# Float64 weights decoded in PSUM, a square moved into the bank of h, and a start on another DMA queue

## The chip, the cores and the metric

The kernel runs on one core of one Trainium2 chip. The metric is the device time of one execution in microseconds. Five engines work side by side, each through its own instructions in a fixed order: TensorE (PE; its weight loads are shown as PEld), VectorE (DVE), ScalarE (ACT), GpSimd (POOL) and SyncE (SP), which issues DMAs. An engine whose next instruction waits for another engine holds up everything behind it in its own order.

## The reference

The program is a causal convolution over the sequence, followed by two MLPs over all 8192 tokens. There are 192 channels and 2048 hidden features, and inputs and outputs are float32; the four weight matrices of the MLPs come as float64.

```python
w = softmax(weight)                       # 8 heads x 7 taps
x = causal_conv(x, w)                     # [8192, 192], one tap row for each 24 channels
h = x @ w_in1;  g = h * clip(h + 3, 0, 6) / 6;  x = g @ w_out1      # layer 1
h = x @ w_in2                                                       # layer 2
P = a0 + a1*h + a2*h**2 + a3*h**3
Q = 1 + |b0|*|h| + |b1|*h**2
out = (P / (Q + 1e-6)) @ w_out2
```

## The kernel before, in words

Tokens go through in 16 blocks of 512 (the last in two halves); activations stay transposed, features on partitions and tokens along the free axis. Each operand of a large product is split into a high and a low part, so that a product is a sum of three: high by high, high by low and low by high. A step is one tile of 128 features: 5 matmuls into h (`mm1`, `mm3`; L464), then element-wise work, then 5 matmuls of its result into the block's accumulators (L478 to L483). In the steady state a step of layer 1 of one block runs beside a step of layer 2 of the block before it: 20 matmuls of 512 columns.

PSUM has four banks of 128x512 for h (`bank0` to `bank3`, printed as bank_93 to bank_96) and four for accumulators. Layer 1 uses banks 0 and 1, layer 2 banks 2 and 3; the second block's layer 1, which runs beside the first's, uses layer 2's banks and buffers. The bank of a step of layer 2 is free for the next product once `G` (L631) has read it.

Layer 2's element-wise work on one tile, by engine: ACT makes A = |h| (L569), in every other tile also a scaled square S (L588), and T = a3*h (L581). POOL makes S = Q - c1 (L602, with L590 ahead of it in every other tile). DVE makes the polynomial in three steps `t2` (L596), `t3` (L607) and `p2` (L626). ACT makes R, 1/sqrt(Q), into A (L612) and squares it to the estimate of 1/Q (`RR`, L617). DVE makes one Newton factor `w` (L622) and the result `G` (L631); ACT rounds it to the high part (`hi2`, L637) and POOL makes the low part (L646). Layer 1's is shorter: `u` (ACT, L506), `g` (DVE, L511), the high part (ACT, L518), the low part (POOL, L524).

The weights arrive as pairs of 32-bit words, 32 tiles of 256, 384 or 512 columns (384 in the mean), through four buffers `raw`. The leading bits of each float64 are put together as a float32 in a tile `m` of SBUF: ACT takes the magnitude of the upper word (L324), DVE clamps it (L332), shifts it (L334) and combines it with sign and lower word (L337, L339); ACT copies the high part (L346 to L355) and POOL (layer 1) or DVE (layer 2) subtracts for the low part (L363). This is done while the first two blocks go through layer 1.

The order of each engine's instructions is not that of the code. Every operation is entered with a time at which it is wanted (tables of offsets such as `OFF`), an estimated length and the buffers it reads and writes, and a planner (`Issue`) writes out one static order; `AHEAD` and `LOOK` say how far it may bring an operation forward. The program's first DMAs are all on SP's queue, the table of taps (`tap`, L840), the softmax row (`line_d`, L845) and the matrices of the convolution made from it (`band`, L266) among the loads of x and of weights.

Of the kernel before, what the change touches and what calls it, by code (L numbers as in the profile page):

```python
# [44 lines left out]
X0 = -2.88  # L45
XW = [-99.782, -93.075, -91.583, -91.01]
BIAS = dict(l1=0.05, dec=-0.28, conv=0.02, out=-0.19, x2=0.95)
AHEAD = dict(P=1.7, A=0.18, V=0.15, G=3.5, S=999)
LOOK = dict(P=29, A=172, V=0, G=1293, S=0)
OFF = dict(  # L50
    sq=0.41, q1=0.596, q2=0.698, mm3=0.072, mm1=0.147, mm4=0.184, tr=0.275, mm2=0.294, A=0.21,
    t1=0.486, u=0.487, R=0.702, RR=0.868, hi2=1.618, hi1=1.431, S=0.271, lo2=2.435, lo1=1.66,
    q=0.669, t2=0.664, t3=1.126, w=1.281, p2=1.267, G=1.367, g=0.622, cv=0.702, x1ah=0.593,
    x1al=1.068, x1bh=0.588, x1bl=0.706, x2ah=0.383, x2al=1.059, x2mh=0.864, x2mc=1.507, x2ml=1.145, oa=0.655,
    oc=0.668, os=0.526, mm2l=0.367, mm4l=0.618,
# [843 lines left out]
```

## Time and profile before

| | |
|---|---|
| median of three runs | 1367.36 us (1365.62, 1367.36, 1374.5) |
| profiled execution: its span, and its time | 1365.6 us, 1365.62 us |
| mean granted TensorE clock | 0.987 |
| busy: PE, DVE, ACT, POOL | 94%, 93%, 87%, 86% |
| first matmul; first product of layer 2 | 17.63 us; 138.25 us |

The span of the profile is the time of that execution, with nothing around it. Matmuls are pipelined, so PE's busy share says little; the distance between the starts of two matmuls says more. Three stages have different limits: the start with the weights (to about 171 us), the steady state (to about 1195 us), and the last block (to the end).

### The profile page before, as it was taken

What the parts mean: (1) busy time and instruction counts of PE and PEld (TensorE: products, weight loads), DVE (VectorE), ACT (ScalarE), POOL (GpSimd) and SP (SyncE); (2) the same over time, 40 slices, a digit from 0 to 9 for tenths busy, and PEclk for the clock granted to TensorE, in tenths of its full rate; (3) what the DMA queues carried; (4) which work ended last, traced back from release to release, by engine and by line L of the source; (5) the groups of instructions that cost most, each with busy time, mean ns of one, the idle gap of its engine ahead of it and who ended that gap; (6) DMA issues with size and microseconds to landing.
All of it is one profiled execution on the core that took longest, in us unless ns stands there. A gap on an engine that the chain in (4) does not pass through costs nothing.

```text
span 1365.6 us, 18227 instructions
## 1 busy us (share of the span) xinstructions
PE 1282.4 (94%) x6048; PEld 1041.8 (76%) x6048; DVE 1269.9 (93%) x1824; ACT 1193.1 (87%) x2174; POOL 1179.1 (86%) x932
## 2 busy tenths in 40 slices
PE   3797999999999999999999999999999999989976
PEld 3574777878788787878888878788787877877776
DVE  6999999999999999999999999999999999998897
ACT  5677899999899999989999989899898989887895
POOL 3665899999999998999989999999999998987886
PEclk9899999999999999999999999999999999999998
DMA  6232000000000000000000000000000000000000
GB/s 197 80 117 70 15 0 13 15 0 27 1 13 1 12 30 12 15 1 12 15 12 16 12 15 12 1 16 12 15 12 1 12 0 6 7 1 12 1 12 12
DMA packets 28983, 28.60 MB, mean 21 GB/s; under 512 B 2140, under 2 KB 25816, under 8 KB 28888
## 3 DMA queue, kind: packets, MB, share of 16 engines
q1 hardware_dynamic: 28888, 27.44, 6.6%
q8 instruction: 47, 0.77, 0.2%
q14 instruction: 48, 0.39, 0.1%
HBM read 21.13 MB, written 6.30 MB: 20 GB/s over the span
## 4 chain that ended last, share of the span: by engine, by line
DVE 46%; PE 33%; ACT 10%; POOL 7%; issue 4%; DMA 1%; SPq 0%; DVEq 0%; POOLq 0%; ACTq 0%
PE bank L464 16%; DVE S L622 11%; DVE bank L626 7%; DVE T L631 6%; DVE u L511 4%; DVE bank L607 4%; DVE T L596 4%; POOL S L602 3%; PE acc L481 3%; PE acc L478 3%; PE acc L479 3%; PE acc L483 3%; PE acc L482 3%; ACT A L617 2%; ACT A L612 2%
## 5 line engine op out<-in xcount | busy, mean ns | idle before, releaser
L602 POOL TENSOR_TENSOR S<-A,S 128x512 f32<-128x512 f32 x252 | 368.5, 1462 | 59.3 <-ACT S L588 43.2
L646 POOL TENSOR_TENSOR g2l<-T,g2h 128x512 fp32r<-128x512 f32 x252 | 326.0, 1294 | 15.0 <-ACT g2h L637 13.9
L524 POOL TENSOR_TENSOR g1l<-u,g1h 128x512 fp32r<-128x512 f32 x240 | 317.9, 1324 | 20.4 <-ACT g1h L518 17.9
L622 DVE SCALAR_TENSOR_TENSOR S<-S,A 128x512 f32<-128x512 f32 x252 | 261.6, 1038 | 13.5 <-ACT A L617 10.0
L626 DVE SCALAR_TENSOR_TENSOR bank<-bank,coef,A 128x512 f32<-128x512 f32 x256 | 192.9, 754 | 38.1 <-ACT A L617 29.7
L637 ACT ACTIVATE g2h<-T 128x512 fp32r<-128x512 f32 x252 | 160.3, 636 | 65.7 <-DVE T L631 64.1
L596 DVE SCALAR_TENSOR_TENSOR T<-T,coef,bank 128x512 f32<-128x512 f32 x252 | 186.8, 741 | 11.4 <-ACT T L581 10.9
L607 DVE SCALAR_TENSOR_TENSOR bank<-T,coef,bank 128x512 f32<-128x512 f32 x252 | 188.2, 747 | 0.7
L631 DVE SCALAR_TENSOR_TENSOR T<-S,bank 128x512 f32<-128x512 f32 x252 | 173.0, 687 | 8.4
L581 ACT ACTIVATE T<-bank,coef 128x512 f32<-128x512 f32 x252 | 173.1, 687 | 1.0 <-POOL g2l L646 0.6
L612 ACT ACTIVATE A<-S 128x512 f32<-128x512 f32 x252 | 158.4, 628 | 15.0 <-POOL S L602 14.4
L617 ACT ACTIVATE A<-A 128x512 f32<-128x512 f32 x256 | 162.1, 633 | 7.5
L511 DVE SCALAR_TENSOR_TENSOR u<-u,bank 128x512 f32<-128x512 f32 x240 | 163.0, 679 | 3.0 <-ACT u L506 2.9
L590 POOL TENSOR_SCALAR S<-A,coef 128x512 f32<-128x512 f32 x126 | 124.9, 991 | 38.5 <-ACT A L569 37.7
L518 ACT ACTIVATE g1h<-u 128x512 fp32r<-128x512 f32 x240 | 150.9, 629 | 2.8 <-DVE u L511 2.6
L506 ACT ACTIVATE u<-bank 128x512 f32<-128x512 f32 x240 | 144.2, 601 | 6.0 <-PE bank L464 3.8
L464 PE MATMUL bank<-x2ah,Ah 128*128 128x512 f32 (+1 forms) x272 | 113.2, 416 | 29.7 <-DVE T L631 24.8
L481 PE MATMUL acc<-g2h,O 128*128 128x512 f32 (+1 forms) x280 | 109.4, 391 | 2.9 <-ACT g2h L637 2.9
L478 PE MATMUL acc<-g2l,O 128*128 128x512 f32 (+1 forms) x280 | 107.8, 387 | 3.6 <-POOL g2l L646 2.4
L464 PE MATMUL bank<-x1ah,Ah 128*128 128x512 f32 (+1 forms) x272 | 105.3, 387 | 5.0 <-DVE T L511 2.2
L482 PE MATMUL acc<-g2h,O 128*128 128x512 f32 (+1 forms) x280 | 107.7, 385 | 0.0
L483 PE MATMUL acc<-g2h,O 128*128 128x512 f32 (+1 forms) x280 | 107.6, 384 | 0.0
(124 smaller groups left out, 3320.3 us busy)
## 6 DMA issues: line engine op xcount, KB each, us to landing
raw<-in_moe_w_out_dram SPq DMA_DIRECT2D x16, 384.0 KB, 3.2
out_dram<-osb SPq DMA_DIRECT2D x32, 192.0 KB, 2.0
xn<-in_x_dram SPq DMA_DIRECT2D x14, 384.0 KB, 3.4
raw<-in_moe_w_in_dram SPq DMA_DIRECT2D x16, 256.0 KB, 3.0
raw<-in_moe_w_in_dram SPq DMA_DIRECT2D x16, 128.0 KB, 3.3
xn<-in_x_dram SPq DMA_DIRECT2D x16, 96.0 KB, 3.3
xn<-in_x_dram SPq DMA_DIRECT2D x2, 288.0 KB, 5.0
band<-line_d SPq DMA_DIRECT2D x1, 512.0 KB, 3.9
```

The costliest lines, as they stand in the source:

```text
L464: nc.tensor.matmul(out=dst[:, cs], lhsT=w[nm][:, fs], rhs=m, start=(k == 0), stop=(k == 4))
L511: stt(out=t, in0=t, scalar=1.0, in1=h1.pop((b, i)), op0=ALU.min, op1=ALU.mult)
L524: nc.gpsimd.tensor_tensor(out=gl, in0=v1.pop((b, i)), in1=f32(g1[b, i][0]), op=ALU.subtract)
L596: stt(out=d["T"], in0=d["T"], scalar=coef[:, 2:3], in1=h2[b, i], op0=ALU.add, op1=ALU.mult)
L602: (nc.gpsimd if k else nc.vector).tensor_tensor(out=d["S"], in0=d["A"], in1=d["S"], op=ALU.add if k == 1 else ALU.mult)
L607: stt(out=h2[b, i], in0=v2[b, i]["T"], scalar=coef[:, 1:2], in1=h2[b, i], op0=ALU.add, op1=ALU.mult)
L612: act(out=d["A"], in_=d["S"], func=ACTF.Abs_reciprocal_sqrt, bias=c1)
L617: act(out=d["A"], in_=d["A"], func=ACTF.Square)
L622: stt(out=d["S"], in0=d["S"], scalar=c1, in1=d["A"], op0=ALU.add, op1=ALU.mult)
L626: stt(out=h2[b, i], in0=h2[b, i], scalar=coef[:, 0:1], in1=v2[b, i]["A"], op0=ALU.add, op1=ALU.mult)
L631: stt(out=d["T"], in0=d["S"], scalar=2.0, in1=h2.pop((b, i)), op0=ALU.subtract, op1=ALU.mult)
L646: e.tensor_tensor(out=gl, in0=v2.pop((b, i))["T"], in1=f32(gh), op=ALU.subtract)
```

## The change

- Weights: the magnitude still goes to a tile `m`, GpSimd clamps it there (`clamp_w`), and DVE's shift writes to one of banks 2 and 3, where the two combining steps follow; high and low parts are taken from there, all low parts by DVE. The 32 tiles take the two banks in turn. The second block's layer 1 has bank 1 to itself, the first block's bank 0.
- Layer 2: `t3` writes T instead of the bank, `RR` writes the bank instead of A, `w` reads S and the bank, and `p2` reads T and the bank.
- `tap`, `line_d`, `band` and the constant matrices are loaded from ScalarE's queue.
- All offsets and the planner's `AHEAD` and `LOOK` are set anew.

```diff
-W1P = [-2.277, -0.017]
+W1P = [-2.0476, -2.171]
-LOENG = [1, 1, 0, 0]
+LOENG = [0, 0, 0, 0]
+CLAMP = [1, 1, 1, 1]
...
     def load_band():
-        nc.sync.dma_start(
+        nc.scalar.dma_start(
...
+    def mag_w(key, k):
         r = raw[key]
         n, t, _ = r
-        r[2] = sgm.tile([128, 512], F32, tag="m", name="m")[:, 0:n]
+        r.append(bank[k][:, 0:n])
+        r[2] = sgm.tile([128, 512], F32, tag="m", name="m")[:, 0:n] if boxed(key) else r[3]
         act(out=r[2], in_=f32(t.rearrange("p (n w) -> p n w", w=2)[:, :, 1]), func=ACTF.Abs)
+    def clamp_w(key):
+        m = raw[key][2]
+        e = 2 * key[1] + (key[0] == "out")
+        (nc.gpsimd if CLAMP[e] else nc.vector).tensor_scalar(out=m, in0=m, scalar1=LIM[0], scalar2=LIM[1],
+                                                             op0=ALU.max, op1=ALU.min)
     def bits_w(key, k):
...
-        if k == 0:
-            nc.vector.tensor_scalar(out=m, in0=m, scalar1=LIM[0], scalar2=LIM[1], op0=ALU.max, op1=ALU.min)
-        elif k == 1:
-            nc.vector.tensor_scalar(out=mi, in0=mi, scalar1=3, scalar2=0x3FFFFFFF,
+        if k == 1:
+            nc.vector.tensor_scalar(out=pi, in0=mi, scalar1=3, scalar2=0x3FFFFFFF,
                                     op0=ALU.logical_shift_left, op1=ALU.bitwise_and)
         elif k == 2:
-            stt(out=mi, in0=t[:, :, 1], scalar=-0x40000000, in1=mi, op0=ALU.bitwise_and, op1=ALU.bitwise_or)
+            stt(out=pi, in0=t[:, :, 1], scalar=-0x40000000, in1=pi, op0=ALU.bitwise_and, op1=ALU.bitwise_or)
         else:
-            stt(out=mi, in0=t[:, :, 0], scalar=29, in1=mi, op0=ALU.logical_shift_right, op1=ALU.bitwise_or)
+            if not LOENG[2 * key[1] + (key[0] == "out")]:
+                r[2], mi = p, pi
+            stt(out=mi, in0=t[:, :, 0], scalar=29, in1=pi, op0=ALU.logical_shift_right, op1=ALU.bitwise_or)
...
     def site1(b, i):
-        return (p2, ("T", "g2h", "g2l"), 2 + i % 2) if b == 1 else (p1, ("u", "g1h", "g1l"), i % 2)
+        if b == 1:
+            return p2, ("T", "g2h", "g2l"), 1
+        return p1, ("u", "g1h", "g1l"), i % 2 if b else 0
...
         def t3(b, i):
-            stt(out=h2[b, i], in0=v2[b, i]["T"], scalar=coef[:, 1:2], in1=h2[b, i], op0=ALU.add, op1=ALU.mult)
+            d = v2[b, i]
+            stt(out=d["T"], in0=d["T"], scalar=coef[:, 1:2], in1=h2[b, i], op0=ALU.add, op1=ALU.mult)
         def RR(b, i):
-            d = v2[b, i]
-            act(out=d["A"], in_=d["A"], func=ACTF.Square)
+            act(out=h2[b, i], in_=v2[b, i]["A"], func=ACTF.Square)
         def w(b, i):
             d = v2[b, i]
-            stt(out=d["S"], in0=d["S"], scalar=c1, in1=d["A"], op0=ALU.add, op1=ALU.mult)
+            stt(out=d["S"], in0=d["S"], scalar=c1, in1=h2[b, i], op0=ALU.add, op1=ALU.mult)
         def p2(b, i):
-            stt(out=h2[b, i], in0=h2[b, i], scalar=coef[:, 0:1], in1=v2[b, i]["A"], op0=ALU.add, op1=ALU.mult)
+            stt(out=h2[b, i], in0=v2[b, i]["T"], scalar=coef[:, 0:1], in1=h2[b, i], op0=ALU.add, op1=ALU.mult)
...
-    at(-62, "S", 475, lambda: nc.sync.dma_start(out=line_d, in_=line), r=[("line", 0)], w=[("line_d", 0)], after=1600)
-    at(-60, "S", 1456, load_band, r=[("line_d", 0)], w=[("band", 0)], after=1700)
-    at(-50, "S", 475, lambda: nc.sync.dma_start(out=perm, in_=ident), w=[("perm", 0)], after=1700)
+    at(-62, "A", 400, lambda: nc.scalar.dma_start(out=line_d, in_=line), r=[("line", 0)], w=[("line_d", 0)], after=1600)
+    at(-60, "A", 400, load_band, r=[("line_d", 0)], w=[("band", 0)], after=3600)
+    at(-50, "A", 400, lambda: nc.scalar.dma_start(out=perm, in_=ident), w=[("perm", 0)], after=3600)
```

How the order of instructions moves is shown at three places.

DVE in the steady state, one step, in the middle of the program. Before (T, S, A are SBUF tiles, bank_95 and bank_96 the two banks of layer 2, u and bank_93 or bank_94 layer 1's):

```order
L631 SCALAR_TENSOR_TENSOR T<-S,bank_95 128x512
L596 SCALAR_TENSOR_TENSOR T<-T,coef,bank_96 128x512
L511 SCALAR_TENSOR_TENSOR u<-u,bank_94 128x512
L607 SCALAR_TENSOR_TENSOR bank_96<-T,coef,bank_96 128x512
L622 SCALAR_TENSOR_TENSOR S<-S,A 128x512
L626 SCALAR_TENSOR_TENSOR bank_96<-bank_96,coef,A 128x512
L631 SCALAR_TENSOR_TENSOR T<-S,bank_96 128x512
```

And with the change (L619 is t2, L631 t3, L530 g, L645 w, L649 p2, L654 G):

```order
L654 SCALAR_TENSOR_TENSOR T<-S,bank_96 128x512
L619 SCALAR_TENSOR_TENSOR T<-T,coef,bank_95 128x512
L631 SCALAR_TENSOR_TENSOR T<-T,coef,bank_95 128x512
L530 SCALAR_TENSOR_TENSOR u<-u,bank_94 128x512
L645 SCALAR_TENSOR_TENSOR S<-S,bank_95 128x512
L649 SCALAR_TENSOR_TENSOR bank_95<-T,coef,bank_95 128x512
L654 SCALAR_TENSOR_TENSOR T<-S,bank_95 128x512
```

The step still holds six instructions; t3 now comes straight behind t2, ahead of layer 1's g, and w has one SBUF and one PSUM operand instead of two SBUF operands.

ACT at the same place, with the engines that each instruction waits for. Before:

```order
L637 ACTIVATE g2h<-T 128x512 [waits DVE_49]
L612 ACTIVATE A<-S 128x512 [waits Activation_49,Pool_49]
L617 ACTIVATE A<-A 128x512 [waits Activation_49]
L569 ACTIVATE A<-bank_95,coef 128x512 [waits PE_49]
L588 ACTIVATE S<-bank_95,root 128x512
```

And with the change:

```order
L660 ACTIVATE g2h<-T 128x512 [waits DVE_49]
L636 ACTIVATE A<-S 128x512 [waits Activation_49,Pool_49]
L640 ACTIVATE bank_96<-A 128x512 [waits DVE_49,Activation_49]
L592 ACTIVATE A<-bank_95,coef 128x512 [waits PE_49]
L611 ACTIVATE S<-bank_95,root 128x512
```

The order is the same; the square (L617, now L640) waits for DVE as well, for t3, the last reader of h in that bank.

ACT at the start of the program. Before:

```order
L857 ACT_TABLE_LOAD
L324 ACTIVATE m<-raw 128x384
L324 ACTIVATE m<-raw 128x512
L346 ACTIVATE O_115<-m 128x2x192
```

And with the change:

```order
L874 DMA tap<-in_weight_dram 8x7
L891 ACT_TABLE_LOAD
L881 DMA perm<-in_ident_dram 128x320
L879 DMA line_d<-line 8x256
L268 DMA band<-line_d 128x8x128
L328 ACTIVATE m<-raw 128x384
```

The issue of band, which waits for line_d to have landed, now stands on ACT, and the first magnitude of the weights stands behind it.

## Rows read from the trace of the kernel before

**Rows 1.** Windows by stage; busy us (count) by engine, granted clock, DMA share.
```profile
core 0: us, PE busy (x) PEld busy (x) DVE busy (x) ACT busy (x) POOL busy (x), PEclk, DMA share, GB/s
...
28.86:138.25 109.39, 85.83 (x359) 65.43 (x359) 106.78 (x179) 77.48 (x167) 66.33 (x57) 0.95 0.29 93
...
171.00:1195.00 1024.00, 1013.68 (x4630) 818.12 (x4629) 968.59 (x1346) 937.27 (x1691) 943.17 (x735) 1.00 0.04 11
1195.00:1365.60 170.60, 142.20 (x867) 124.56 (x865) 147.36 (x211) 137.30 (x245) 133.69 (x106) 0.93 0.03 8
```

**Rows 2.** Groups by line: busy us, mean ns | idle before, releaser.
```profile
L622 DVE SCALAR_TENSOR_TENSOR S<-S,A 128x512 f32<-128x512 f32 x252 | 261.6, 1038 | 13.5 <-ACT A L617 10.0
...
L631 DVE SCALAR_TENSOR_TENSOR T<-S,bank 128x512 f32<-128x512 f32 x252 | 173.0, 687 | 8.4
L581 ACT ACTIVATE T<-bank,coef 128x512 f32<-128x512 f32 x252 | 173.1, 687 | 1.0 <-POOL g2l L646 0.6
...
L617 ACT ACTIVATE A<-A 128x512 f32<-128x512 f32 x256 | 162.1, 633 | 7.5
```

**Rows 3.** Timeline (start, length) of steady steps, DVE and POOL rows.
```profile
705.24 0.68 DVE L622 SCALAR_TENSOR_TENSOR S<-S,A 128x512 f32<-128x512 f32 x1
...
714.02 1.31 POOL L646 TENSOR_TENSOR g2l<-T,g2h 128x512 fp32r<-128x512 f32 x1
...
714.25 1.63 DVE L622 SCALAR_TENSOR_TENSOR S<-S,A 128x512 f32<-128x512 f32 x1
```

**Rows 4.** Waits from 171 to 1195 us: total, times, longest.
```profile
PEld bank L464 <- DVE T L631: 37.0, 72, 1.3
...
DVE bank L626 <- ACT A L617: 21.3, 50, 1.2
```

**Rows 5.** Chain of waits, ten matmuls of 512 columns.
```profile
721.05 2.27 PE bank L464 x10
```

**Rows 6.** Groups by line of DVE from 0 to 171 us.
```profile
L339 DVE SCALAR_TENSOR_TENSOR m<-raw,m 128x384 int32<-128x384 int32 (+2 forms) x32 | 25.9, 821 | 0.1
L337 DVE SCALAR_TENSOR_TENSOR m<-raw,m 128x384 int32<-128x384 int32 (+2 forms) x32 | 25.9, 820 | 0.2
L332 DVE TENSOR_SCALAR m<-m 128x384 f32<-128x384 f32 (+2 forms) x32 | 18.2, 577 | 3.7 <-ACT m L324 3.6
...
L334 DVE TENSOR_SCALAR m<-m 128x384 int32<-128x384 int32 (+2 forms) x32 | 16.1, 513 | 0.1
...
L363 DVE TENSOR_TENSOR O<-m,O 128x256 fp32r<-128x256 f32 (+1 forms) x16 | 7.4, 501 | 0.0
L363 DVE TENSOR_TENSOR Al<-m,Ah 128x256 fp32r<-128x256 f32 x8 | 7.0, 871 | 0.0
...
L363 DVE TENSOR_TENSOR Bl<-m,Bh 64x256 fp32r<-64x256 f32 x8 | 4.4, 548 | 0.1
```

**Rows 7.** Timeline of DVE, first decoded tile, POOL idle.
```profile
7.58 0.36 DVE L334 TENSOR_SCALAR m<-m 128x384 int32<-128x384 int32 x1
7.98 0.56 DVE L337 SCALAR_TENSOR_TENSOR m<-raw,m 128x384 int32<-128x384 int32 x1
```

**Rows 8.** Timeline of DVE beside POOL in the weight stage.
```profile
33.27 1.48 POOL L524 TENSOR_TENSOR g1l<-u,g1h 128x512 fp32r<-128x512 f32 x1 [0.83 <-ACT g1h L518]
...
33.51 1.39 DVE L332 TENSOR_SCALAR m<-m 128x256 f32<-128x256 f32 x1
```

**Rows 9.** Timeline of the DMA queue and the first product.
```profile
7.49 0.30 SPq L845 DMA_DIRECT2D line_d<-line  x1
...
10.70 0.38 SPq L314 DMA_DIRECT2D raw<-in_moe_w_out_dram  x1
...
13.61 0.38 SPq L266 DMA_DIRECT2D band<-line_d  x1
...
17.63 3.63 PE L411 MATMUL bank<-xn,band 128*122 128x120 f32 x16 [17.63 <-DVE m L337]
```

**Rows 10.** Waits from 1195 us to the end.
```profile
PE bank L464 <- DVE T L631: 15.2, 11, 2.9
```

More of the change, by code (lines that the diff above doesn't have):

```diff
@@ L20 @@
 CONV = -11
+CONV2 = 1.7151
 PAT = [1, 2]
@@ L44 @@
 D2T = 5
[L45 to L49, printed above, removed]
-OFF = dict(
[L51 to L55, printed above, removed]
+X0 = -3.5576
+XW = [-98.6812, -95.7871, -90.8177, -84.1979]
+BIAS = dict(l1=1.5372, dec=1.797, conv=1.4061, out=-0.7086, x2=3.0264)
+AHEAD = dict(P=4.733, A=25.052, V=17.217, G=15.336, S=999.0)
+LOOK = dict(P=3, A=156, V=132, G=410, S=0)
+OFF = dict(
+    sq=-0.2391, q1=-0.0381, q2=0.2567, mm3=-0.423, mm1=0.8404, mm4=0.4459, tr=0.6018, mm2=0.8241, A=-0.3233,
+    t1=0.075, u=0.9885, R=0.5331, RR=0.6369, hi2=1.4938, hi1=1.9951, S=-0.1322, lo2=1.926, lo1=2.8291,
+    q=-3.2594, t2=0.1782, t3=0.4844, w=0.7884, p2=0.8597, G=0.9565, g=1.2626, cv=0.9616, x1ah=1.0094,
+    x1al=1.7783, x1bh=1.0281, x1bl=1.2078, x2ah=1.7232, x2al=2.0125, x2mh=1.2801, x2mc=2.4281, x2ml=1.7914,
+    oa=0.6663, oc=0.8609, os=1.4993, mm2l=1.1909, mm4l=0.5848,
 )
@@ L679, in words_of, with weights @@
         return 384 if kind == "out" else 256 if c % 2 else 512
-    def weights(t_load, t, kind, l, c):
+    def weights(t_load, t, kind, l, c, turn):
         key = (kind, l, c)
         n = words_of(kind, c)
-        m = ("m" if wide else "raw", key)
-        at(t_load, "S", 728 if n == 256 else 1775 if n == 512 else 1092, load_w, *key, w=[("raw", key)], after=1700)
+        side = 2 * l + (kind == "out")
+        bk = (f"bank{2 + turn % 2}", ("w", key))
+        m = ("raw", key)
+        at(t_load, "S", 1050 if n == 256 else 2100 if n == 512 else 1570, load_w, *key, w=[("raw", key)], after=1900)
         if wide:
-            at(t, "A", n * 0.835 + 93, mag_w, key, r=[("raw", key)], w=[m], kind="dec")
-            for k in range(4):
-                at(t + WPART["v0"] + WPART["vs"] * k, "V", n * (0.53 if k < 2 else 1.045) + 66, bits_w, key, k,
-                   r=[("raw", key), m] if k > 1 else [m], w=[m], kind="dec")
-        g = "G" if LOENG[2 * l + (kind == "out")] else "V"
+            box, m = ("m", key), bk
+            first = [box] if boxed(key) else [bk]
+            at(t, "A", n * 0.835 + 93, mag_w, key, 2 + turn % 2, r=[("raw", key)], w=first, kind="dec")
+            at(t + WPART["c0"], "G" if CLAMP[side] else "V", n * 1.49 + 90 if CLAMP[side] else n * 1.045 + 126, clamp_w, key,
+               w=first, kind="dec")
+            for k in range(1, 4):
+                r = [("raw", key)] if k > 1 else first
+                w = [bk]
+                if k == 3 and LOENG[side]:
+                    r, w, m = r + [bk], [box], box
+                at(t + WPART["v0"] + WPART["vs"] * k, "V", n * 1.045 + (126 if w == [bk] else 66), bits_w, key, k,
+                   r=r, w=w, kind="dec")
+        g = "G" if LOENG[side] else "V"
         for part in range(1 if n < 512 else 3):
             if kind == "out":
-                ns, hi, lo = (413, 1104 if g == "G" else 550), ("Oh", l, c), ("Ol", l, c)
+                ns, hi, lo = (413, 1104 if g == "G" else 467), ("Oh", l, c), ("Ol", l, c)
             elif part == 0:
@@ L723, in transient @@
         else:
-            k = fill[0] % 2 if t < 0 else 1 - [k for w, k in line1 if w <= t][-1]
+            k = fill[0] % 2 if t < 0 else 0 if t < steps[0] else 1 - [k for w, k in line1 if w <= t][-1]
             fill[0] += 1
@@ L810, in conv_moe_moe_kernel @@
         if not b * C % S:
-            at(-97 + b if first else t - 9, "V", 207, zero_x, b, w=[("xn", b)])
-        at(-96 + b if first else t - 8, "S", 1500, load_x, b, w=[("xn", b)], after=1700)
+            at(-101 + b if first else t - 9, "V", 207, zero_x, b, w=[("xn", b)])
+        at(-100 + b if first else t - 8, "S", 1900, load_x, b, w=[("xn", b)], after=1700)
         where = {nm: OFF[nm] for nm in ("tr", "cv", "x1ah", "x1al", "x1bh", "x1bl")}
         step = 1.0
-        if first:
-            where, step = dict(tr=0.0, cv=0.01, x1ah=0.01, x1al=0.02, x1bh=0.01, x1bl=0.02), 0.1
+        if t < steps[0]:
+            t += 0.0 if first else CONV2
+            where, step = dict(tr=0.0, cv=0.01, x1ah=0.01, x1al=0.02, x1bh=0.01, x1bl=0.02), 0.1 if first else 1.0
         for hf in range(2):
@@ L831, in conv_moe_moe_kernel @@
         tiles.append((W1P[0] + 2 * c, "in", 0, c))
-        tiles.append((W1P[0] + W1P[1] + 2 * c, "out", 0, c))
+        tiles.append((W1P[1] + 2 * c, "out", 0, c))
         tiles.append((W2P[0] + 2 * c, "in", 1, c))
-        tiles.append((W2P[0] + W2P[1] + 2 * c, "out", 1, c))
+        tiles.append((W2P[1] + 2 * c, "out", 1, c))
     tiles.sort()
     for k, v in enumerate(tiles):
-        weights(XW[k] if k < rings["raw"] else tiles[k - rings["raw"]][0] + WPART["v0"] + 3 * WPART["vs"] + 0.001, *v)
+        weights(XW[k] if k < rings["raw"] else tiles[k - rings["raw"]][0] + WPART["v0"] + WPART["vs"] * 3 + 0.001, *v, k)
     at(-99, "A", 1900, nc.scalar.preload_act_table, ACTF.Abs_reciprocal_sqrt)
-    at(-99, "S", 475, lambda: nc.sync.dma_start(out=tap, in_=weight), w=[("tap", 0)], after=1600)
+    at(-99.5, "A", 400, lambda: nc.scalar.dma_start(out=tap, in_=weight), w=[("tap", 0)], after=1600)
     at(-98, "V", 274, lambda: nc.vector.memset(line, 0.0), w=[("line", 0)])
```

41 lines of the change are left out of this document (22 added, 19 removed).

## The prediction

> **What bounds the kernel now.** I read the busy time by stages first, then the groups by line, then single steps in the timeline, and last who waited for whom. The stages have to be taken apart, because the page's shares (PE 94%, DVE 93%) mix them [rows 1].
>
> In the steady state, 171 to 1195 us, TensorE issues a matmul of 512 columns every 0.227 us: ten took 2.27 us [rows 5]. 4630 matmuls [rows 1] at that distance would be 1051 us, more than the window's 1024, since some are small ones of the convolution and the transposes. So PE is close to its own rate there, and only its waits can be won back. The largest by far is for G, the last reader of layer 2's bank: 37.0 us in 72 waits [rows 4]. DVE, on which G stands, is busy 968.6 of 1024 us [rows 1].
>
> What makes G late is `w`. It takes 1038 ns in the mean, while G itself, a like instruction with one operand in the bank, takes 687 [rows 2]. The reader is to see why in the steps: alone, `w` took 0.68 us; the one that began at 714.25 took 1.63. At that time a POOL instruction ran from 714.02 to 715.33, and `w` ended at 715.88, 0.55 us later [rows 3]: it did nothing until POOL was through. `w` is the one instruction of the step with both inputs in SBUF.
>
> In the stage of the weights, 28.86 (first product of layer 1) to 138.25 us (first of layer 2), DVE is busy 106.8 of 109.4 us, ACT 77.5, POOL 66.3, and PE issues 359 matmuls, at most 81.5 us at 0.227 [rows 1]. DVE is the bound. The weights take 104.9 us of it up to 171 us, the sum of seven groups [rows 6], and these wait for POOL too: a clamp of 256 columns that began at 33.51 took 1.39 us, to 34.90, behind a POOL instruction from 33.27 to 34.75 [rows 8]; with POOL idle, a shift of 384 columns took 0.36 and a combining step 0.56 us [rows 7].
>
> **The change, part by part.**
>
> *Layer 2.* `w` gets a PSUM operand. Its new price lies between the 0.68 us that it takes alone [rows 3] and today's 1.038; I take G's 687 ns, the same operands [rows 2]. That is 351 ns by 252 tiles, 88 us of DVE time, of which some 74 lie in the steady window (1024 of the 1227 us that follow 138.25, so some 210 tiles). It is no gain by itself, since PE has no 74 us to give; the gain is the share of the 37.0 us [rows 4] that ends. 351 ns are two thirds of the mean wait (37.0 / 72 = 0.51 us), and the worst `w`, with 0.95 us of waiting, fall away whole. I take 24 us. The ends are 5 (another wait takes its place) and 32 (only what several late instructions in a row cause is left).
>
> [...] By the row, an operand in PSUM costs nothing: G with the bank takes 687 ns, `w` alone from SBUF 0.68 us [rows 2, 3]. [...] The row is of this kernel, and I go by it.
>
> `t3` and `p2` only swap places of operands (T and the bank, as `t2` has them now); nothing is charged. `RR` now writes PSUM, of which the trace has no ACT row; the nearest are 633 ns (SBUF to SBUF) and 687 (PSUM to SBUF) [rows 2]. I take 633; the ends are 54 ns less or more, 14 us of ACT's time over 252 tiles, and ACT has 87 us idle in the steady window [rows 1]. If that cover were gone, the 14 us would come back in part on the chain of w. `RR` also waits for `t3` now. Behind it on ACT stand the next tile's A, S and T and layer 1's u; `w` waits for it. In the new order DVE does `g` (one instruction) between `t3` and `w`, about as long as the square's 633 ns, so the wait is nearly covered. I charge nothing here and keep it as a rival.
>
> *Weights.* Today DVE spends 104.9 us [rows 6]. Then: 32 clamps go to POOL; 32 shifts and 64 combining steps have one SBUF and one PSUM operand, so by the argument above they no longer wait for POOL. A combining step is priced at its 0.56 us alone, at the mean size of 384 columns. A shift alone is 0.36 now, but no row has it into PSUM; between 0.36 and the 0.56 of a two-operand instruction I take the upper end [rows 7]. 96 by 0.56 is 53.8 us. [...] Together 80, that is 25 us less, some 22 of it inside the stage: DVE 106.8 - 22 = 85. PE's 81.5 and ACT's 77.5 are then as long. Three engines of equal load that feed each other do not fit into the longest; with a tenth on top the stage takes 93, a gain of 16. Ends: 4 (the two banks for 32 tiles, and one bank instead of two for each block's layer 1, hold them back) and 26 (85 reached). POOL loses half of the subtractions and gets the clamps, and has 43 us idle in the stage.
>
> *Start.* The first product of the convolution starts at 17.63 us, 4.0 us after band was issued on SP at 13.61, although line_d was issued at 7.49; loads stand between them, one issued at 10.70 [rows 9]. On ACT only perm stands ahead, and band can follow at about 10 to 11. The first magnitude then waits behind band on ACT, which delays the first weight tile by some 2 us of DVE work. I take 3 us of gain, between 0 and 4.
>
> *Last block.* From 1195 us PE waits 15.2 us for G [rows 10]. With some 35 tiles left (252 less 210 in the steady state and the first few), `w` saves 12 us of DVE; the new order there is not one that rows can price. I take 6, between 0 and 14.
>
> The sum: 24 + 16 + 3 + 6 = 49. The profiled execution took 1365.6 us, 1.8 below the median of the runs; 1365.6 - 49 = **1317 us**. By the least of each term (5 + 4) it is 1357, by the most (32 + 26 + 4 + 14) 1290.
>
> **The rivals.**
>
> 1. *The steady state gives nothing* (1344 us): `w` runs at 0.69, but waits for the square as long as it waited for POOL. For it: DVE already waits 21.3 us for that square, at p2 [rows 4]. Against: ACT's order is the same. 1365.6 - 16 - 3 - 2 = 1344.
> 2. *Everything falls into place* (1290): the sum of the upper ends. For it: POOL too is freed, as the instruction that both engines want is gone.
> 3. *The weights stay the bound and nothing else helps* (1358): each tile holds one of two banks from the shift to the last low part, and ACT's up to seven copies of a tile stand in between; then DVE waits where it worked. With 5 us from the steady state and 3 from the start it is 1358.
> 4. *Slower* (1398): `RR` behind `t3` stretches each step. A step is 4.88 us (1024 us for some 210 tiles, 252 by 1024 / 1227), and DVE works 968.6 / 210 = 4.61 of it, 4.26 without the 351 ns, so that 0.62 is free. Up to that a wait before `w` is covered; from there it decides. If R starts only when `t3` ends, R and the square are 1.27 us, of which `g`, priced as G, covers 0.69: a wait of 0.58. If one more ACT instruction of 0.63 stands ahead in two of five steps, the mean is 0.83: 0.21 by 252 is 53 us lost, less 19 from the start and the weights and 2 from the last block: 32 more than now.
>
> That `w` is not shortened by the bank at all leads to the first rival's time.
>
> **How the numbers follow.** Chances: forecast 0.50 (its own range 1303 to 1335), first rival 0.17, second 0.18, third 0.09, slower 0.06. From no change a measurement of this kernel tells about 1%, 13.7 us. Faster than 1353.7: 0.50 + 0.17 + 0.18 + 0.01 of the third = 0.86; within 1%: 0.08 of the third; slower by over 1%: 0.06. The range runs from 1288, below the second rival, to 1353, above the first; it leaves out the third and the fourth and a little below.
>
> **What would show it.** `w`'s group at 0.68 to 0.72 us, with none near 1.6; POOL's groups shorter; PE's wait for G under half of 37 us. The combining steps near 0.56 us in the mean; layer 2's first product near 119 us instead of 138.25; the first product of the convolution before 15 us. Wrong would be a new large wait of DVE's `w` for ACT's square, or of DVE's shift for ACT's copies of the weights.

## The result and the profile after

The changed kernel takes 1337.46 us in the median of four runs (1334.66 to 1338.3), the kernel before 1368.87 us in its four (1365.62 to 1374.5). The ratio is 0.977, with an interval of 0.9743 to 0.9798. The forecast was 1317 us, the range 1288 to 1353. The profiled execution has a span of 1332.8 us, 32.8 less than before, where the sum of the terms was 49. Its time is 1334.66 us, 1.9 above that span, while for the kernel before the two agree; by the medians the gain is 31.4.

First the stages of the changed kernel (columns as in [rows 1]).

```profile
28.86:138.25 109.39, 98.30 (x418) 75.66 (x419) 95.55 (x199) 86.83 (x185) 88.09 (x67) 0.99 0.31 94
171.00:1195.00 1024.00, 1014.62 (x4715) 831.70 (x4714) 917.01 (x1363) 946.59 (x1709) 895.71 (x745) 1.00 0.04 11
1195.00:1333.00 138.00, 113.77 (x709) 99.56 (x707) 116.41 (x175) 112.29 (x201) 103.58 (x88) 0.95 0.03 9
```

In the same 1024 us PE issues 85 matmuls more than in [rows 1], and DVE is busy 51.6 us less. The stages themselves are best bounded by products with `x2ah`, layer 2's input, since a fixed window holds other work in the two kernels. The 138.25 us that the text ahead calls the first product of layer 2 is its third matmul (the first with `x2al`); the first begins 1.7 us earlier, and the stage of the weights took 107.7 us (136.59 - 28.86), not 109.4. Here are the first product and the first matmul of layer 2's 209th step of 272 (the 14th block's first), before and then after (start, length):

```profile
136.59 0.50 PE L464 MATMUL bank<-x2ah,Ah 128*128 128x512 f32 x1 [3.91 <-ACT x2ah L535]
...
1135.51 0.39 PE L464 MATMUL bank<-x2ah,Ah 128*128 128x512 f32 x1
```

```profile
126.49 0.39 PE L481 MATMUL bank<-x2ah,Ah 128*128 128x512 f32 x1
...
1109.33 0.39 PE L481 MATMUL bank<-x2ah,Ah 128*128 128x512 f32 x1
```

So layer 2 begins 10.1 us earlier, and its 209th step 26.2 earlier. At the end it is 32.8. The first product of layer 1 begins at 28.68 instead of 28.86. The gain in these two profiles is thus 0.2 us in the start, 10 in the weight stage, 16 in the steady state and 6.6 in the last part. The 16 repeats: between those two matmuls lie 998.9 us before and 982.8 after, and 982.6 to 983.9 in the six kernels below that leave layer 2 as the change has it. Start and weight stage repeat less well, as told at the end.

The groups that answer to [rows 2] (busy us, mean ns | idle before, releaser), and the square, whose price was open:

```profile
L645 DVE SCALAR_TENSOR_TENSOR S<-S,bank 128x512 f32<-128x512 f32 x252 | 172.8, 686 | 85.5 <-ACT bank L640 83.0
L654 DVE SCALAR_TENSOR_TENSOR T<-S,bank 128x512 f32<-128x512 f32 x252 | 173.1, 687 | 8.5
L640 ACT ACTIVATE bank<-A 128x512 f32<-128x512 f32 x256 | 154.2, 603 | 14.7 <-DVE T L631 8.7
```

`w` (L645) now costs what `G` (L654) does, 686 ns; the longest of the 252 took 692, where 64 took over 1.5 us before. But 85.5 us of idle time stand ahead of it, nearly all for ACT's square. The timeline shows that POOL no longer holds it up; `w` begins inside a POOL instruction, as in [rows 3], and takes 0.69:

```profile
710.37 1.28 POOL L543 TENSOR_TENSOR g1l<-u,g1h 128x512 fp32r<-128x512 f32 x1
...
710.55 0.69 DVE L645 SCALAR_TENSOR_TENSOR S<-S,bank 128x512 f32<-128x512 f32 x1 [0.55 <-ACT bank L640]
```

POOL gains as well, as rival 2 had it. Its instruction S = A times S (or plus S), before and then after, is shorter by 165 ns in the mean:

```profile
L602 POOL TENSOR_TENSOR S<-A,S 128x512 f32<-128x512 f32 x252 | 368.5, 1462 | 59.3 <-ACT S L588 43.2
```

```profile
L625 POOL TENSOR_TENSOR S<-A,S 128x512 f32<-128x512 f32 x252 | 326.9, 1297 | 57.7 <-ACT S L611 45.2
```

Who waited for whom from 171 to 1195 us (total, times, longest):

```profile
DVE S L645 <- ACT bank L640: 70.2, 134, 1.2
...
PEld bank L481 <- DVE T L654: 10.2, 18, 1.4
PEld acc L495 <- POOL g2l L669: 6.1, 13, 0.8
ACT bank L640 <- DVE T L631: 5.8, 22, 0.3
...
PEld bank L481 <- ACT osb L693: 3.5, 4, 1.2
...
PEld acc L498 <- ACT g1h L537: 2.8, 5, 1.5
...
PEld bank L481 <- ACT x1n L436: 1.7, 4, 0.8
```

PE's wait for G, 37.0 us in [rows 4], is 10.2. Other waits of PE have grown beside it: the sum of all its PEld rows goes from 42.7 only to 28.8. The chain that ended last says the same. Before, DVE made up 46% of it and PE 33%; after it is

```profile
PE 73%; DVE 9%; ACT 9%; POOL 5%; issue 3%; DMA 0%; ACTq 0%; DVEq 0%; POOLq 0%
```

The weights on DVE, 0 to 171 us, which answer to [rows 6], and the clamps on POOL:

```profile
L349 DVE TENSOR_SCALAR bank<-m 128x384 int32<-128x384 int32 (+2 forms) x32 | 17.8, 555 | 10.2 <-POOL m L337 9.5
L356 DVE SCALAR_TENSOR_TENSOR bank<-raw,bank 128x384 int32<-128x384 int32 (+2 forms) x32 | 17.7, 554 | 0.2
L352 DVE SCALAR_TENSOR_TENSOR bank<-raw,bank 128x384 int32<-128x384 int32 (+2 forms) x32 | 17.7, 553 | 0.1
L380 DVE TENSOR_TENSOR O<-bank,O 128x256 fp32r<-128x256 f32 (+1 forms) x32 | 9.9, 350 | 0.1
L380 DVE TENSOR_TENSOR Al<-bank,Ah 128x256 fp32r<-128x256 f32 x16 | 6.7, 421 | 5.4 <-ACT Bl L372 2.2 <-ACT Bh L370 2.2 <-ACT Ah L365 1.0
L380 DVE TENSOR_TENSOR Bl<-bank,Bh 64x256 fp32r<-64x256 f32 x16 | 6.7, 421 | 3.9 <-ACT Bl L372 1.9 <-ACT Bh L370 1.7
```

```profile
L337 POOL TENSOR_SCALAR m<-m 128x384 f32<-128x384 f32 (+2 forms) x32 | 47.5, 1495 | 24.4 <-ACT m L328 18.6 <-ACT coef L277 5.5 <-PE bank L481 0.3
```

DVE's groups sum to 76.5 us (104.9 before). A clamp takes 1495 ns in the mean on POOL, and was 577 on DVE [rows 6], waits for POOL included.

### The profile page after: what moved, and what is told of

The parts are those of the page before. It is cut to its first block, busy times and chain, and to the rows that moved or that the text cites. A ratio compares the mean times of both kernels' runs of the same rounds, so it can differ in the third digit from the quotient of the medians.

```text
span 1332.8 us, 18555 instructions
## 1 busy us (share of the span) xinstructions
PE 1268.9 (95%) x6048; PEld 1042.9 (78%) x6048; DVE 1172.6 (88%) x1824; ACT 1188.3 (89%) x2174; POOL 1127.3 (85%) x932
## 4 chain that ended last, share of the span: by engine, by line
PE 73%; DVE 9%; ACT 9%; POOL 5%; issue 3%; DMA 0%; ACTq 0%; DVEq 0%; POOLq 0%
PE bank L481 35%; PE acc L495 7%; PE acc L498 7%; PE acc L500 7%; PE acc L499 7%; PE acc L496 7%; PE bank L428 2%; DVE S L645 1%; DVE bank L649 1%; POOL g2l L669 1%; POOL S L625 1%; DVE T L654 1%; ACT bank L640 1%; POOL g1l L543 1%; PE bank L443 1%
## 5 line engine op out<-in xcount | busy, mean ns | idle before, releaser
L625 POOL TENSOR_TENSOR S<-A,S 128x512 f32<-128x512 f32 x252 | 326.9, 1297 | 57.7 <-ACT S L611 45.2
L543 POOL TENSOR_TENSOR g1l<-u,g1h 128x512 fp32r<-128x512 f32 x240 | 312.0, 1301 | 26.3 <-ACT g1h L537 21.2
L645 DVE SCALAR_TENSOR_TENSOR S<-S,bank 128x512 f32<-128x512 f32 x252 | 172.8, 686 | 85.5 <-ACT bank L640 83.0
L631 DVE SCALAR_TENSOR_TENSOR T<-T,coef,bank 128x512 f32<-128x512 f32 x252 | 188.5, 748 | 8.8
L619 DVE SCALAR_TENSOR_TENSOR T<-T,coef,bank 128x512 f32<-128x512 f32 x252 | 187.0, 742 | 8.6 <-ACT T L604 7.2
L649 DVE SCALAR_TENSOR_TENSOR bank<-T,coef,bank 128x512 f32<-128x512 f32 x252 | 188.7, 749 | 0.0
L654 DVE SCALAR_TENSOR_TENSOR T<-S,bank 128x512 f32<-128x512 f32 x252 | 173.1, 687 | 8.5
L530 DVE SCALAR_TENSOR_TENSOR u<-u,bank 128x512 f32<-128x512 f32 x240 | 162.7, 681 | 16.5 <-ACT u L525 15.3
L640 ACT ACTIVATE bank<-A 128x512 f32<-128x512 f32 x256 | 154.2, 603 | 14.7 <-DVE T L631 8.7
L613 POOL TENSOR_SCALAR S<-A,coef 128x512 f32<-128x512 f32 x126 | 97.9, 777 | 43.1 <-ACT A L592 42.1
L481 PE MATMUL bank<-x2ah,Ah 128*128 128x512 f32 (+1 forms) x272 | 106.4, 391 | 16.9 <-DVE T L654 16.6
L495 PE MATMUL acc<-g2l,O 128*128 128x512 f32 (+1 forms) x280 | 112.6, 404 | 4.2 <-POOL g2l L669 2.3
L498 PE MATMUL acc<-g2h,O 128*128 128x512 f32 (+1 forms) x280 | 109.4, 391 | 0.1
```

What stands on the lines that cost most here:

```text
L481: nc.tensor.matmul(out=dst[:, cs], lhsT=w[nm][:, fs], rhs=m, start=(k == 0), stop=(k == 4))
L495: nc.tensor.matmul(out=a, lhsT=o[:, 0:128], rhs=g, start=False, stop=sp)
L498: nc.tensor.matmul(out=a, lhsT=o[:, 0:128], rhs=g, start=st, stop=False)
L543: nc.gpsimd.tensor_tensor(out=gl, in0=v1.pop((b, i)), in1=f32(g1[b, i][0]), op=ALU.subtract)
L619: stt(out=d["T"], in0=d["T"], scalar=coef[:, 2:3], in1=h2[b, i], op0=ALU.add, op1=ALU.mult)
L625: (nc.gpsimd if k else nc.vector).tensor_tensor(out=d["S"], in0=d["A"], in1=d["S"], op=ALU.add if k == 1 else ALU.mult)
```

## The experiments: layer 2

Times are medians of four runs. Each ratio is to the kernel before on the same chip, whose median was 1369.1, 1371.1 or 1369.5 us, with the 95% interval behind it. The theory (A) was that the PSUM operand of `w` is the gain of the steady state.

**d1_w_sbuf**: the old places in the changed kernel; the planner sees it and sets the order anew. The edit in short form (output <- inputs):

```diff
-  t3: T <- T, bank          RR: bank <- A    w: S <- S, bank   p2: bank <- T, bank
+  t3: bank <- T, bank       RR: A <- A       w: S <- S, A      p2: bank <- bank, A
```

> The changed kernel with layer 2's operands placed as before: the square in A in SBUF, t3 in the bank, so that w reads S and A, both in SBUF. Weights, queues and offsets as changed. Theory A (an instruction of DVE with two SBUF inputs waits for a running GpSimd instruction, and the steady gain is w's): w goes from 0.686 back to 0.95 to 1.05 us in the mean, with single ones near 1.6; the time goes up by 10 to 20 us, from 1337 to about 1350. Rival B (the steady gain is that of the new offsets): w gets longer all the same, but the time stays within 4 us of 1337.

Measured: 1426.27 us, ratio 1.0414 (1.0398 to 1.0431). `w` takes 1198 ns and PE's wait for G is 97.1 us. The direction of theory A was right, the size far off (about 1350 was expected): the kernel is slower than the one before, which has the same four instructions. The places alone do not explain that, and the order had changed too.

**d2_w_p2_sbuf**: in the changed kernel only the square stays in A, so that both `w` and `p2` read two SBUF operands. The planner sets the order anew here too.

```diff
-  RR: bank <- A    w: S <- S, bank    p2: bank <- T, bank
+  RR: A <- A       w: S <- S, A       p2: bank <- T, A
```

> The changed kernel with the square in A in SBUF and t3 in T in SBUF, so that w (S and A) and p2 (T and A) both have two SBUF inputs: the suspected cost doubled. Theory A: both at 0.95 to 1.1 us in the mean; DVE's step goes from 4.3 to about 4.9 us, over the 4.74 us that a step takes in the changed kernel, so DVE becomes the bound and the time goes up far more than with one such instruction: 1375 to 1430. Rival C (an SBUF operand has its own price, with no waiting): both instructions get longer by a constant, single ones do not reach 1.5 us, and the time stays under 1365.

Measured: 1582.14 us, ratio 1.1542 (1.1517 to 1.1567); `w` 1200 ns, `p2` 1229 (749 in the change), PE's wait for G 177.2 us. Rival C is out, and theory A's upper end is passed by 152 us. The second instruction with two SBUF operands gets longer by about as much as the first (480 and 514 ns), and adds 156 us to d1's time, where the first added 89 to the change's. Why so much more is not shown: part of both sums is the planner's new order.

**d1o_order_kept**: the edit of d1, but every engine keeps the order of the changed kernel, so that the place is all that differs.

> The changed kernel with every engine's order of instructions left as it is, and only the four instructions of layer 2 put back where they were (t3 writes the bank, the square stays in A, w reads S and A, p2 reads the bank and A). Theory A (the PSUM operand of w is the gain of the steady state, whatever the order): w 1.0 to 1.2 us in the mean, PE's wait for G from 171 to 1195 us above 37 us, time 1355 to 1400. Rival C (the loss of d1_w_sbuf came from the order, which the planner had set anew for it): 1345 or less.

Measured: 1394.75 us, ratio 1.0192 (1.0176 to 1.0208): theory A. `w` takes 1175 ns, and PE's wait for G is 51.0 us. A step in its timeline:

```profile
702.38 1.29 POOL L543 TENSOR_TENSOR g1l<-u,g1h 128x512 fp32r<-128x512 f32 x1
...
702.44 1.78 DVE L645 SCALAR_TENSOR_TENSOR S<-S,A 128x512 f32<-128x512 f32 x1
...
707.81 0.69 DVE L645 SCALAR_TENSOR_TENSOR S<-S,A 128x512 f32<-128x512 f32 x1 [0.15 <-ACT A L640]
```

Again `w` ends 0.55 us after POOL's instruction (704.22 and 703.67), as in [rows 3]; with POOL idle it takes 0.69. The 57 us between this kernel and the change are the worth of the place in the new order. The rest of d1's loss (1426.27 - 1394.75 = 32 us) came with the planner's new order.

**b1o_place_only**: the other half, the new places in the kernel before, all orders as they are. In the old order `p2` often stands ahead of `w`, which then reads p2's result instead of the square; the values are changed, the instructions are the same in kind; b2 below has the right ones.

> The kernel before with its orders of instructions left as they are, and only the four instructions of layer 2 in the places of the change (w reads S and the bank). Theory A: w 0.68 to 0.72 us, PE's wait for G from 171 to 1195 us down to 15 to 25 us, time 11 to 19 us under the kernel before, 1350 to 1358. Rival E (the new order is needed, since the square now waits for t3, which in the old order stands directly ahead of w): w waits for the square 100 us or more, PE's wait for G stays at 37 us or grows, and the time is that of the kernel before or above it.

Measured: 1426.38 us, ratio 1.0423 (1.0406 to 1.0441). `w` takes 688 ns, as theory A has it, and yet the kernel loses 57 us: rival E. Only its 100 us at `w` are not met there: `w` waits 42.3 us for the square, and `p2`, where it stands ahead, 81.2. From 171 to 1195 us:

```profile
ACT bank L617 <- DVE T L608: 120.8, 165, 1.3
PEld bank L464 <- DVE T L631: 89.1, 156, 1.2
```

ACT waits 120.8 us with its square for `t3` (L608), where in the changed kernel it was 5.8.

**b2_place_t3_first**: the same places, declared to the planner, so that `p2` stands behind `w` and the values are right. Besides the places, two offsets change:

```diff
-  t3=1.126, w=1.281, p2=1.267      (last block: p2=1.401)
+  t3=0.75,  w=1.281, p2=1.29       (last block: p2=1.43)
```

> The kernel before with the four instructions of layer 2 in the places of the change, declared so to the planner, and in its tables only what this needs: t3 wanted before the square (0.75 instead of 1.126; 0.868 is the square's), p2 after w (1.29 instead of 1.267, in the last block 1.43 instead of 1.401). All other offsets, the weights and the start as before. In the order that comes out t3 still stands directly ahead of w, behind g. Theory E (the square's wait for t3 eats what w gains as long as t3 stands late): ACT waits for t3 at the square 80 us or more in all, w 0.69 us, time 1385 to 1430. Theory A (declared rightly, the PSUM operand pays by itself): 1350 to 1360.

Measured: 1435.63 us, ratio 1.0458 (1.0432 to 1.0483), theory E with its upper end passed; `w` 687 ns, ACT's wait for t3 124.0 us. The timeline shows one step, with `g` (L511), a part of the next block's input (L440), `t3` (L608), the square (L617) and `w` (L622):

```profile
700.76 0.69 DVE L511 SCALAR_TENSOR_TENSOR u<-u,bank 128x512 f32<-128x512 f32 x1 [0.23 <-ACT u L506]
...
701.48 0.69 DVE L440 TENSOR_TENSOR x1b<-bank,x1b 64x512 fp32r<-64x512 f32 x1
...
702.20 0.75 DVE L608 SCALAR_TENSOR_TENSOR T<-T,coef,bank 128x512 f32<-128x512 f32 x1
...
703.04 0.60 ACT L617 ACTIVATE bank<-A 128x512 f32<-128x512 f32 x1 [1.27 <-DVE T L608]
...
703.75 0.69 DVE L622 SCALAR_TENSOR_TENSOR S<-S,bank 128x512 f32<-128x512 f32 x1 [0.81 <-ACT bank L617]
```

With `t3` behind these two, ACT stands idle 1.27 us for it, then DVE 0.81 us for the square: the two engines wait in turn.

**p_pad_w**: the changed kernel with a DVE instruction of 0.27 us ahead of each `w`, where DVE waits for the square.

```diff
+            nc.vector.memset(line, 0.0)
             stt(out=d["S"], in0=d["S"], scalar=c1, in1=h2[b, i], op0=ALU.add, op1=ALU.mult)
```

> The changed kernel with one more DVE instruction directly ahead of each w: it zeroes a row buffer that is no longer needed, 8 by 256, 0.27 us, 252 times, 69 us of DVE's time in all; all orders kept. Theory H (DVE's 70.2 us of waiting for the square at w are slack, and PE's own rate is what bounds the steady state): 0 to 8 us slower than the changed kernel, 1337 to 1345, and DVE's wait at w falls by 40 us or more. Rival I (G still reaches PE by the chain through w): 25 to 60 us slower, PE's wait for G at 37 us or more.

Measured: 1339.79 us, ratio 0.9789 (0.9774 to 0.9803): theory H. The whole program's groups, and the wait from 171 to 1195 us:

```profile
L646 DVE SCALAR_TENSOR_TENSOR S<-S,bank 128x512 f32<-128x512 f32 x252 | 166.4, 660 | 38.0 <-ACT bank L640 35.5
L645 DVE MEMSET line<- 8x256 f32 x256 | 69.6, 272 | 1.2
```

```profile
DVE S L646 <- ACT bank L640: 28.7, 70, 1.0
```

69.6 us more work on DVE cost 2.3 us, no more than the medians scatter. `w` waits 41.5 us less than in the changed kernel, so at least that much of its 70.2 us was spare time.

## The experiments: weights and start

**c_mul_add**: the clamp as a product by 1 and a sum with 0, which leaves the limits on the weights out.

```diff
-    scalar1=LIM[0], scalar2=LIM[1], op0=ALU.max, op1=ALU.min
+    scalar1=1.0, scalar2=0.0, op0=ALU.mult, op1=ALU.add
```

> The changed kernel, its clamp on GpSimd with multiply by 1 and add 0 in place of max and min: the same shapes, in place, two immediates, but no clamping. Theory D (max and min are what makes the clamp 1.5 us on GpSimd): the clamp falls to 0.6 to 0.8 us in the mean of 384 columns, GpSimd's 47.5 us of clamps to about 22, and the start gets 3 to 8 us shorter: about 1332. Rival E (the form, in place with immediates, has that price): still 1.5 us, time within 2 us of 1337.

Measured: 1332.89 us, ratio 0.9734 (0.9719 to 0.9748), theory D, with a clamp shorter than its 0.6 to 0.8 us. The price was in the two operations:

```profile
L337 POOL TENSOR_SCALAR m<-m 128x384 f32<-128x384 f32 (+2 forms) x32 | 16.3, 515 | 37.2 <-ACT m L328 27.1 <-ACT coef L277 8.4 <-PE bank L481 1.7
```

**c_max_mul**: a maximum and a product by 1 (no upper limit).

```diff
-    scalar2=LIM[1], op0=ALU.max, op1=ALU.min
+    scalar2=1.0,    op0=ALU.max, op1=ALU.mult
```

> The changed kernel with only the lower bound kept in GpSimd's clamp: a maximum and then a product by 1 instead of a maximum and a minimum (the upper bound on the weights is left out); all orders kept. Theory L (each maximum or minimum has its own price, half of the 980 ns between 515 and 1495): the clamps take 1.0 us in the mean, first product of layer 2 at 125.5 to 126.5 us, time 1333 to 1337. Rival M (one such operation in the instruction is enough to make all of it slow): 1.45 to 1.5 us, time as that of the changed kernel, 1336 to 1339. Rival N (only the pair is slow): 0.5 us, time 1332 to 1334.

Measured: 1336.74 us, ratio 0.9766 (0.9747 to 0.9785), rival M:

```profile
L337 POOL TENSOR_SCALAR m<-m 128x384 f32<-128x384 f32 (+2 forms) x32 | 47.6, 1496 | 25.0 <-ACT m L328 17.7 <-ACT coef L277 7.1 <-PE bank L481 0.3
```

One maximum, with a product behind it, makes the whole instruction as slow as both, 1496 ns against 1495 with a minimum behind it and 515 with a product and a sum; a pair other than product and sum, but without a maximum or minimum, was not tried.

**c_none**: no clamps at all (the limits on the weights are left out); the planner orders what remains.

> The changed kernel without the clamps (weights outside float32's range would not be held in it): 32 GpSimd instructions, 47.5 us, and one engine less on each weight tile's way. Theory F (GpSimd's clamps are what kept the weight stage from its forecast): layer 2's first product comes 5 to 12 us earlier than at 126.5 us, time about 1328. Rival G (ACT's copies and the two banks set that stage): within 3 us of 1337.

Measured: 1330.56 us, ratio 0.9714 (0.97 to 0.9729). Its weight stage, from the first product of layer 1 to the first of layer 2, and the same stage of the changed kernel:

```profile
31.40:123.50 92.10, 84.05 (x366) 66.30 (x367) 82.61 (x181) 76.96 (x169) 43.06 (x34) 0.99 0.35 107
```

```profile
28.68:126.49 97.81, 86.72 (x367) 66.27 (x367) 84.28 (x182) 76.96 (x167) 80.03 (x61) 0.98 0.35 106
```

DVE, ACT and PE do nearly the same in both, POOL 43.06 instead of 80.03 us, and the stage is 5.7 us shorter: theory F in the main. In c_mul_add, which keeps the order, the stage (29.43 to 125.35 us) takes 95.9, 1.9 less than with the change. Layer 2 began 3.0 us earlier here, under the 5 to 12 expected, since layer 1 began 2.7 later.

**c_dve_clamp** and **c_mix_clamp**: all clamps on DVE, or those of layer 1 only; the planner knows of it and may move what stands around them.

```diff
-CLAMP = [1, 1, 1, 1]
+CLAMP = [2, 2, 2, 2]      # 1: GpSimd, 2: DVE;  c_mix_clamp: [2, 2, 1, 1]
```

> The changed kernel with the 32 clamps on DVE instead of GpSimd, in the tile m of SBUF. Theory J (DVE bounds the stage of the weights, GpSimd does not): the clamps take 0.45 to 0.6 us on DVE, 14 to 19 us in all, against DVE's 9.5 us of waiting for GpSimd's clamps, so the first product of layer 2 starts at 128 to 136 us and the time is 1339 to 1347. Rival K (GpSimd's 1.5 us clamps bound the stage): first product of layer 2 at 122 to 125 us, time 1329 to 1334.

> The changed kernel with layer 1's 16 clamps on DVE, so that the first tiles need not wait for 1.5 us each of GpSimd, and layer 2's 16 left on GpSimd. Theory J: half of the cost, time 1337 to 1342. Rival K: first product of layer 1 one to two us earlier than in the changed kernel and the time 1330 to 1335, under the changed kernel.

Measured: 1342.53 us, ratio 0.9781 (0.9759 to 0.9802), and 1335.97 us, 0.9736 (0.9716 to 0.9757). With all on DVE they take 19.7 us there (625 ns, above the 0.45 to 0.6 expected), and layer 2 starts at 136.1: theory J. DVE is then busy 100.6 us of a stage of 105.9 (30.19 to 136.13 us). With half, layer 2 starts at 129.4 in the profile, later than with the change, but the time is not above it; neither theory's numbers are met, and the interval overlaps that of the change. No version that keeps both limits is measurably faster than the change.

**s_queue_back**: the first four DMAs on SP's queue again, orders kept.

```diff
-        nc.scalar.dma_start(      # tap, line_d, band, constant matrices
+        nc.sync.dma_start(
```

> The changed kernel with orders kept, and only the four first DMAs (taps, softmax row, band, constant matrices) back on SyncE's queue, each at the place in it that the order gives. Theory F (the queue is worth nothing, because the first block's products wait for weights and not for band): first product of layer 1 within 1 us of the changed kernel, time 1334 to 1340. Rival G (the queue brings what was forecast): first product of the convolution 2 us or more later, time 1340 to 1343.

Measured: 1338.03 us, ratio 0.9775 (0.976 to 0.979). Its start, and that of the changed kernel:

```profile
4.65 0.54 ACT L328 ACTIVATE m<-raw 128x384 f32<-128x384 f32 x1 [2.64 <-DMA raw<-in_moe_w_out_dram]
...
12.66 0.38 SPq L268 DMA_DIRECT2D band<-line_d  x1
...
16.85 3.63 PE L428 MATMUL bank<-xn,band 128*122 128x120 f32 x16 [16.85 <-DMA band<-line_d]
```

```profile
5.64 0.31 ACTq L879 DMA_DIRECT2D line_d<-line  x1
...
10.91 0.41 ACTq L268 DMA_DIRECT2D band<-line_d  x1
...
11.37 0.54 ACT L328 ACTIVATE m<-raw 128x384 f32<-128x384 f32 x1 [8.70 <-DMA line_d<-line]
...
15.50 3.35 PE L428 MATMUL bank<-xn,band 128*122 128x120 f32 x16 [15.50 <-DVE bank L356]
...
19.51 1.26 PE L443 MATMUL bank<-perm,x1n 122*128 122x122 f32 x10 [0.66 <-ACT x1n L436]
...
22.27 3.39 PE L428 MATMUL bank<-xn,band 128*122 128x120 f32 x16 [1.50 <-DVE x1al L454]
```

The change gets band out 1.75 us earlier, and pays with the first magnitude, 6.7 us later. Theory F's time was met, not its place: layer 1 began at 30.91, 2.2 us later, though kernels with the change's start have it anywhere from 28.7 to 30.3. At the end 0.6 us was left, less than can be measured.

## Why the prediction was right, and where it was not

**Steady state, 24 expected, 16 measured: the term that was mis-sized most.** The mechanism was right: `w` at 686 ns, its wait for POOL gone, PE's wait for G down by 26.8 us. The step that failed is the one from that wait to time: the prediction put the share of the 37.0 us that ends at 24, near the fall that came, and took all of it as gain. The PEld rows show what took its place: the wait for POOL's low part `g2l` went from nothing to 6.1 us, for `osb` to 3.5, for `g1h` from 0.6 to 2.8, for `x1n` to 1.7. The sum of PE's waits fell by 13.9 us, near the 16. An engine that has several suppliers gains from one of them only until the next is last.

**The new wait of `w`** was named as a sign that the forecast is wrong. It came (70.2 us), and is none: DVE is busy 51.6 us less in the window, and waits for the square 40.5 us more than it did at `p2` (21.3 in [rows 4]) and at `w` together:

```profile
DVE S L622 <- ACT A L617: 8.4, 12, 0.8
```

An engine's freed time must show up as idle time somewhere; p_pad_w shows that most of it is spare. In d1o the same account holds the other way: `w` is longer by (1175 - 686) x 252 = 123 us, its idle time shrinks by 54 (from 83.0 to 28.6), and of the 69 that remain 57 come out as time.

**The square behind `t3`, charged nothing: right, and only because of the order.** The argument was that `g` between `t3` and `w` covers it, and ACT waits 5.8 us. With `t3` behind `g`, in b1o and b2, the slower rival is what happens: 1426 and 1436 us, where it was put at 1398, or 1419 without the 21 us of gains elsewhere that those two lack. Places and order together make the gain:

| | old places | new places |
|---|---|---|
| orders of the kernel before | 1368.87 | 1426.38 |
| orders of the change | 1394.75 | 1337.46 |

The lower row has the new weights and start as well. In the upper right field `w` often reads a wrong value; b2, which reads the right one, has 1435.63. Each half alone is slower than before. The square itself takes 603 ns into PSUM, below the 633 taken and inside the bounds of 54 ns. The operand in PSUM cost `w` nothing, as [rows 2] and [rows 3] had it: 686 ns with the bank, and 0.69 us alone from SBUF (d1o_order_kept).

**Weights, 16 expected, 10 measured.** The working for DVE held: 76.5 us against 80, and in the stage 84.28 against 85; shift and combining steps at 0.55 against 0.56. The 80 has 26 us in it for the low parts, which no run shows; in the changed kernel they took 23.3 (9.9 + 6.7 + 6.7), 0.42 us for 256 columns and 0.28 for 128. What failed is the sentence on POOL, which "loses half of the subtractions and gets the clamps": that was charged nothing, and 47.5 us came, nearly three times what a product and a sum of that size take (16.3 us, c_mul_add). POOL's load in the stage rose to 80 us, a fourth engine near the bound. Without the clamps the stage takes 92.1 us, 15.6 less than before, the gain that was forecast. Single profiles scatter here: with the change's instructions the stage takes 97.8 us in the change, 98.3 in p_pad_w, 99.3 in c_max_mul and 101.9 in d1o_order_kept, against 107.7 before, so the 10 may be as little as 6.

**Start, 3 expected, 0.2 by the first product of layer 1.** Band was issued at 10.91, as foretold, and the convolution began 2.1 us earlier, but at 15.50, not before 15. The change's row, under s_queue_back, names the first decoded tile (L356) as what came last, but the convolution does not read it: with SP's queue that tile was ready at 8.65, and the product waited for band until 16.85. In p_pad_w, whose start is the change's, the row names band:

```profile
15.66 3.63 PE L428 MATMUL bank<-xn,band 128*122 128x120 f32 x16 [15.66 <-DMA band<-line_d]
```

So band took 4.6 us and more from its issue, where 4.0 were counted. The first tile paid more than the 2 us charged: DVE was done with it at 15.38 us, and at 9.13 before. The lead of 2.1 us was then used up: PE waited 1.50 and 1.09 us for `x1al` from DVE, where it was 0.89 and 0.90, and the second block's convolution took 3.39 us, and before:

```profile
24.07 1.97 PE L411 MATMUL bank<-xn,band 128*122 128x120 f32 x16 [0.89 <-DVE x1al L437]
```

From 22 to 26 us the granted clock was 1.00 before and 0.59 after, with 0.50 in each of the three microseconds from 22 to 25. PE had stood idle 1.50 us ahead of it after and 0.89 before. What set the clock was not tried, and it is not the whole: in c_max_mul this convolution took 1.97 us after the same 1.50 of idle time, and layer 1 began at 29.41. In b1o_place_only, with the old start, it began at 27.91. The new queue is worth nothing that these runs can tell.

**Last block, 6 expected, 6.6 measured, in part by luck.** From the 209th step to the end the waits for G at PE's weight loads are 17.8 us, and were 21.8; all such waits together are 31.2, and were about 35. The granted clock of that part is 0.97, and was 0.95; it was 1.00 but for some stretches, in which it went down to 0.50 (after, from 1319 to 1325 us; before, from 1224 to 1230). Its first fall there came at 1298 and at 1223 us, and in the microsecond ahead of it PE was busy 0.00 us in both kernels. By an estimate 0.02 of 223 us is 4 us; the prediction has no term for it, and what raised the clock was not tried.

## What to carry to other kernels

Here a PSUM operand freed a DVE instruction from a busy GpSimd (686 ns in the mean with it, 1175 without, in the same order), but the instruction that then filled the bank had to wait for the bank's last reader (from 171 to 1195 us 5.8 us with that reader early, 120.8 and 124.0 with it late): move that reader forward in the order, or the gain turns into a loss (57 and 65 us here). Before taking a wait as gain, list the engine's other suppliers, and take the difference of the sums. Measure the price of an operation on the engine to which it is moved, since the clamp cost nearly three times what a multiply and add cost there (1495 and 515 ns).

## What the runs showed of the hardware

- On GpSimd the tensor-scalar instruction with a maximum and a minimum took 1067, 1495 and 1923 ns for 256, 384 and 512 columns (the changed kernel); with a product and a sum 406, 515 and 624 ns (c_mul_add). One maximum, followed by a product, is enough: 1071, 1496 and 1923 ns (c_max_mul).
- DVE's `w` with two SBUF operands took 0.69 us with GpSimd idle and 1.78 beside a GpSimd instruction (d1o_order_kept); with one of them in PSUM none of 252 took over 692 ns (the changed kernel). `w` and `p2` both with two SBUF operands cost 245 us, the planner's new order included (d2_w_p2_sbuf against the change).
- GpSimd's product or sum of two SBUF tiles got shorter by the same move, 1297 ns in the mean in the changed kernel instead of 1462 in the kernel before (1417 in d1o_order_kept).
- ScalarE's square of 512 columns took 603 ns into PSUM (the changed kernel) and 630 to 633 into SBUF (d1o_order_kept, the kernel before).
